# First-layer weight conversion on VectorE and ScalarE, even pieces for the band's values, and a new order of steps

## The chip, the core and the metric

One core of a Trainium2 chip runs the whole program. The metric is the device time of one execution in microseconds (us), as the median over several runs. The core has five engines that work through queues of their own, in order: TensorE (PE; its weight loads are listed as PEld), VectorE (DVE), ScalarE (ACT), GpSimd (POOL) and SyncE (SP), which here issues every DMA transfer. An instruction that waits holds up all that stand behind it on its engine.

## What is computed

The reference is an attention over two scales and two dense layers (the weights come as float64, all else as float32):

```python
# q, k, v: (4, 8, 576, 64)
q_d, k_d, v_d = means of 4 neighbours along the sequence      # 144 long
out = repeat(softmax(q_d k_d^T / 8) v_d, 4)                   # dense, pooled
    + softmax(q k^T / 8 where |i - j| < 4, else -1e9) v       # the band
x = out, heads side by side                                   # (2304, 512)
x = silu(x @ w_in) @ w_out                                    # 512 -> 2048 -> 512
x = h * sigmoid(1.702 h) @ w2_out,  h = x @ w2_in             # the same sizes
```

## The kernel before

**Stages.** The 2304 tokens are taken as eight half sequences of 288 (m = 0 to 7) in the first layer and as six blocks of 384 in the second. Attention is done in 32 *units*, one for each half sequence and pair of heads; four units (a half sequence) give the input of one first-layer block. A unit goes PE (transposes of q and k, L946 and L913; scores `sl`, L965 and L971), DVE (L979 to L988), POOL (subtract the maximum, L994), ACT (exponentials, L1000 and L1004), DVE (sums, L1007 to L1015), POOL (divide, L1018), DVE (transpose, L1033), PE (`ul`, L1042 and L1048), ACT (L1054), DVE (`xf`, L1062 and L1063, and its maximum, L1066). After four units the input is split into two float16 halves, `xhl` (L682 on ACT, L685 on DVE).

**The dense layers.** Each product is made of three float16 matmuls. A block's first product goes to PSUM as `hps` (L605); ACT takes its tanh (L617), DVE multiplies (L620), ACT and DVE split the result (`g`, L624 and L627); the second product is `ops` (L718, for m = 0 L746 with additions by DVE in L760; second layer L780). All of block m = 0 waits for the first layer's weights.

**Weights.** A weight comes as the two 32-bit words of a float64. `conv` (L295 to L327) makes a float32 out of them on integers: ACT scales the high word (L302) and converts the low word (L306, into `z`), DVE shifts the high word left by 3 (L310), DVE takes the sign bit into the upper half of `z` (L315), and POOL adds the two as integers (L319). The first layer's weights go through in 16 pieces of 128 x 1024 words (`weights1`), the second layer's in 32 pieces of 128 x 512 (`weights2`), which also pass through DRAM. `halves` then makes the float16 halves: ACT the upper (L338), DVE the rest (L342).

**The band.** A block of 24 queries sees 32 keys. `first_key` moves the window of the first and last block inward at the edges, so there are three masks (`bigs`), and `load_vw` fetches the values in eight DMAs for each pair of heads: 12, 12, 2, 5, 5, 2, 5, 5 windows of 32 keys.

**Order.** Every step of the program is an entry of `Plan`. A table of digits, `PLACES`, sets the one global order in which the steps are written out; every engine then executes its share in that order. SP's DMAs stand in it too.

Of the kernel before, what the change touches and what calls it, by code (L numbers as in the profile page):

```python
# [19 lines left out]
NEG = -1.0e9  # L20
# [3 lines left out]
BAND = 4  # L24
TERMS = ((0, 0), (0, 1), (1, 0))
# [7 lines left out]
    "0e0h0i0l0k0n0s0t0v0u0I0L0w0M0T0W1y0f0o0r0O0g0m0x0J0N0P0S0Q0U0X0Y100Z15171c1g1o1A2c14161d1E13181e1f1l1k1n1m1p1B1C1F1H1M1W1N202i2p2r1K"
    "1U1O2m1J1T1P1Z2a2b2g2f2h2n2o2q2s2y2z2u2A2C2F2G2K2M2N2R2W313g3J4w5m6h6M8o2527495e2L2Q2O2V2Z30393c3z3K3L3S3P4b4i3T4K4N4X4Z33383e3r403I"
    "4k3R4f4z4A4U4G5g5x5G5N5Q5T6i5058525h5o5n5y5v5P5Z6063666e6q6j6u6D6J6L5W68626c6k6m6r6p6C6G6H6K6I6Q6X6N6Y71797a7E7J7N858s8v8X3o467A5f6y"
    "6z6w7v7B927t7y959U9W967c7i7p4T7d7j7q7F7M7L7T7O7Y8a8b8f8c8k8D8u8G8J8N9l7X81897r7U7Z888i8n8t8C8w8K8O8P8S8Q8V9g8Z9v9A9EaD8U9c909G8T9b8Y"
# [28 lines left out]
    "B8BeBhBiBkBpBjBlBmBnBuBwBoBrBsBtBvBx"
)


class Rec:
    pass  # L70

class Step:
    __slots__ = ("name", "eng", "dur", "fn", "deps", "succ", "keys", "alloc", "lock", "rank", "start", "end", "left", "n", "mb")


class Plan:


    def __init__(self, caps):
        self.steps, self.last, self.readers, self.tags, self.users = [], {}, {}, {}, {}
        self.soft = []
        self.caps = caps

    def add(self, name, eng, dur, fn, r=(), w=(), alloc=(), lock=False, mb=0.0, after=()):
        s = Step()
# [110 lines left out]
def kernel(ctx: ExitStack, tc: tile.TileContext, q, k, v, w1_in, w1_out, w2_in, w2_out, out):  # L198
# [1081 lines left out]
```

## Time and profile before

| | |
|---|---|
| median of 3 runs (lowest, highest) | 946.28 us (944.89, 947.38) |
| span of the profiled execution | 945.0 us |
| median less that span | 1.3 us |
| busy PE, DVE, ACT, POOL | 885.7, 501.2, 422.6, 167.4 us |

The profile is of one execution. A busy PE is one with a matmul under way; small matmuls overlap, so a busy PE can still be short of its full rate. The granted TensorE clock is given as a share of 2.4 GHz. A row of a line gives its count, busy time and mean duration; a row of the order of time gives start and duration.

### The profile page before, as it was taken

What the parts mean: (1) busy time and instruction counts of PE and PEld (TensorE: products, weight loads), DVE (VectorE), ACT (ScalarE), POOL (GpSimd) and SP (SyncE); (2) the same over time, 40 slices, a digit from 0 to 9 for tenths busy, and PEclk for the clock granted to TensorE, in tenths of its full rate; (3) what the DMA queues carried; (4) which work ended last, traced back from release to release, by engine and by line L of the source; (5) the groups of instructions that cost most, each with busy time, mean ns of one, the idle gap of its engine ahead of it and who ended that gap; (6) DMA issues with size and microseconds to landing.
All of it is one profiled execution on the core that took longest, in us unless ns stands there. A gap on an engine that the chain in (4) does not pass through costs nothing.

```text
span 945.0 us, 20792 instructions
## 1 busy us (share of the span) xinstructions
PE 885.7 (94%) x8926; PEld 592.3 (63%) x8926; DVE 501.2 (53%) x1033; ACT 422.6 (45%) x753; POOL 167.4 (18%) x165
## 2 busy tenths in 40 slices
PE   4567789999999999999999999999999999999998
PEld 2335566777777777777778776455455464554553
DVE  5789999885857728537372557506025043140230
ACT  4668776776765526334251356315023132240230
POOL 4645542435342102301100000000000000000000
PEclk9997799999999999999999999999999999999999
DMA  7885346566655121311050030000000000000001
GB/s 191 261 260 195 91 132 170 167 188 221 182 173 151 43 65 39 86 26 36 2 224 1 2 125 10 12 23 1 22 12 1 23 1 1 34 1 34 1 1 45
DMA packets 87228, 76.85 MB, mean 81 GB/s; under 512 B 66912, under 2 KB 71520, under 8 KB 86112
## 3 DMA queue, kind: packets, MB, share of 16 engines
q1 hardware_dynamic: 87136, 75.52, 26.6%
q8 instruction: 70, 1.15, 0.5%
q14 instruction: 22, 0.18, 0.1%
HBM read 62.39 MB, written 13.11 MB: 80 GB/s over the span
## 4 chain that ended last, share of the span: by engine, by line
PE 76%; DVE 13%; ACT 4%; DMA 3%; POOL 2%; issue 2%; SPq 0%; POOLq 0%; ACTq 0%; DVEq 0%
PE hps L605 34%; PE ops L780 20%; PE ops L718 16%; DMA st<-in_moe_w_in_dram 2%; PE ul L1048 1%; DVE z L315 1%; DVE win L342 1%; DVE g L627 1%; PE sl L971 1%; DVE tg L620 1%; PE ul L1042 1%; DVE wout L342 1%; PE sl L965 1%; DMA vraw<-in_v_dram 1%; ACT st L302 1%
## 5 line engine op out<-in xcount | busy, mean ns | idle before, releaser
L605 PE MATMUL hps<-xhl,win 128*128 128x288 f16 (+1 forms) x2688 | 399.7, 309 | 12.3 <-DVE tg L620 10.4
L605 PEld LDWEIGHTS <-win 128*128 128x128 f16 x2688 | 264.3, 100 | 130.7 <-issue 11.2
L620 DVE SCALAR_TENSOR_TENSOR tg<-tg,hps 128x576 f32<-128x576 f32 (+1 forms) x112 | 93.3, 833 | 237.6 <-ACT tg L617 237.5
L780 PE MATMUL ops<-wout,g 128*128 128x512 f16 x864 | 187.8, 379 | 0.0
L718 PE MATMUL ops<-g,wout 128*128 128x288 f16 x1344 | 169.7, 286 | 1.0 <-DVE tg L620 1.0
L718 PEld LDWEIGHTS <-wout 128*128 128x128 f16 x1344 | 130.2, 98 | 33.8 <-DVE tg L620 1.4
L617 ACT ACTIVATE tg<-hps,blk 128x576 f32<-128x576 f32 (+1 forms) x112 | 90.6, 808 | 132.5 <-PE hps L605 126.9
L780 PEld LDWEIGHTS <-g 128*128 128x128 f16 x864 | 84.5, 98 | 100.9
L791 ACT ACTIVATE o<-ops,blk 128x512 f32<-128x512 f32 x18 | 12.4, 687 | 155.2 <-PE ops L780 155.2
L627 DVE SCALAR_TENSOR_TENSOR g<-tg,g 128x768 f16<-128x768 f32 (+1 forms) x56 | 51.0, 924 | 13.9 <-ACT g L624 13.8
L624 ACT ACTIVATE g<-tg 128x768 f16<-128x768 f32 (+1 forms) x56 | 44.8, 814 | 27.3 <-DVE tg L620 27.3
L319 POOL TENSOR_TENSOR cs<-cs,cz 128x512 int32<-128x512 int32 x32 | 43.2, 1354 | 51.1 <-DVE cz L315 18.8
L627 DVE SCALAR_TENSOR_TENSOR g<-tg,gs,g 128x576 f16<-128x576 f32 x56 | 48.0, 864 | 6.5 <-ACT g L624 6.5
L624 ACT ACTIVATE g<-tg,gs 128x576 f16<-128x576 f32 x56 | 42.5, 769 | 7.9 <-DVE tg L620 7.9
L319 POOL TENSOR_TENSOR x<-x,z 128x1024 int32<-128x1024 int32 x16 | 41.0, 2568 | 23.1 <-DVE x L310 7.0
L994 POOL TENSOR_TENSOR sc<-sc,mx 128x192 f32<-128x192 f32 x32 | 18.7, 584 | 148.6 <-DVE mx L988 146.1
L302 ACT ACTIVATE st<-st 128x512 f32<-128x512 f32 (+1 forms) x48 | 39.5, 827 | 9.3 <-DMA st<-in_moe_w_in_dram 7.3
L1018 POOL TENSOR_TENSOR sc<-sc,smr 128x192 f32<-128x192 f32 x32 | 23.0, 719 | 82.4 <-DVE smr L1012 76.9
L1000 ACT ACTIVATE pd<-sl,nm 72x144 f32<-72x144 f32 x64 | 23.5, 371 | 31.2 <-DVE sc L985 25.2
L728 ACT ACTIVATE x<-ops,blk 128x576 f32<-128x576 f32 x14 | 10.3, 738 | 40.5 <-PE ops L718 40.5
L1054 ACT ACTIVATE us<-ul 128x288 f32<-128x288 f32 x32 | 13.1, 409 | 34.2 <-PE ul L1048 34.0
L746 PE MATMUL ops<-g,wout 128*128 128x288 f16 x192 | 26.7, 294 | 1.6 <-DVE x L760 1.0
(122 smaller groups left out, 845.8 us busy)
## 6 DMA issues: line engine op xcount, KB each, us to landing
st<-in_moe_w_in_dram SPq DMA_DIRECT2D x8, 1024.0 KB, 7.5
st<-in_moe_w_out_dram SPq DMA_DIRECT2D x8, 1024.0 KB, 5.0
st<-in_moe_w_in_dram SPq DMA_DIRECT2D x16, 512.0 KB, 4.5
st<-in_moe_w_out_dram SPq DMA_DIRECT2D x16, 512.0 KB, 5.8
vraw<-in_v_dram SPq DMA_DIRECT2D x16, 288.0 KB
kraw<-in_k_dram SPq DMA_DIRECT2D x32, 144.0 KB, 4.0
qraw<-in_q_dram SPq DMA_DIRECT2D x64, 72.0 KB, 3.2
out_dram<-o SPq DMA_DIRECT2D x18, 256.0 KB, 2.0
```

The costliest lines, as they stand in the source:

```text
L302: ACT.activation(out=hi.bitcast(F32), in_=hi.bitcast(F32), func=AF.Copy, scale=2.0 ** -112)
L319: POOL.tensor_tensor(out=s, in0=s, in1=zget(), op=ALU.add)
L605: nc.tensor.matmul(o, T[w][:, kc, a, fc * P:(fc + 1) * P], T[xk][:, kc, b, :T_], start=(n == 0), stop=(n == 3 * KC - 1))
L617: ACT.activation(out=T[tg], in_=T[ps][:, :, :T_], func=AF.Tanh, scale=T["a" + bk][:, c:c + 1])
L620: DVE.scalar_tensor_tensor(out=T[tg], in0=T[tg], scalar=1.0, in1=T[ps][:, :, :T_], op0=ALU.add, op1=ALU.mult)
L624: ACT.activation(out=T[g][:, 0], in_=T[tg], func=AF.Copy, scale=gs)
L627: DVE.scalar_tensor_tensor(out=T[g][:, 1], in0=T[tg], scalar=gs, in1=T[g][:, 0], op0=ALU.mult, op1=ALU.subtract)
L718: nc.tensor.matmul(o, w[:, j, a, dc * P:(dc + 1) * P], g[:, b, j % 2, :], start=(n == 0), stop=(n == 3 * NF - 1))
L746: nc.tensor.matmul(T[ps][:, i, :HALF], T[f"wout1.{c}"][:, j, a, dc * P:(dc + 1) * P], g[:, b, j % 2, :], start=(n == 0), stop=(n == 11))
L780: nc.tensor.matmul(o, g[:, a, j % 2, t * P:(t + 1) * P], w[:, j, b, :], start=(i == 0), stop=(i == 3 * NF - 1))
L1000: ACT.activation(out=T[pd][:, hh, :], in_=sd()[:, hh, :], func=AF.Exp, bias=T[nmx][:, hh:hh + 1], scale=SCD, accum_out=T[sr][:PD, 6 + hh:7 ...
L1018: POOL.tensor_tensor(out=scu(), in0=scu(), in1=T["smr"][u % 2][:, 0:6].unsqueeze(2).to_broadcast([P, 6, 32]), op=ALU.mult)
```

## The change

For the first layer's weights the sign bit is taken by ACT (`sg`: the scaled high word, which is tiny, is written as float16, where only the sign is left) in place of DVE's `cg`, and the integer add is made by DVE (`cd`) in place of POOL's `cp`. The second layer keeps the old way. The keys in SBUF get 4 columns of zeros at either end, so that every window starts at its regular place; one mask is enough, and the cap's two edge blocks are closed by two small memsets. The band's values come in four DMAs of 32 partitions x 12 windows (five for the first and last pair of heads, with a small memset by POOL). `PLACES` is a new table: all steps may stand elsewhere. The durations that the steps carry do not set the order; the table alone does.

```diff
+CONV = {"in": [("DVE", "ACT")] * 8, "out": [("DVE", "ACT")] * 8}
 PLACES = (
-    "000b020104050A030D1s0E1u211t0C0G1w23060p0q0y0z111i0B0K0V0R1b121h0F1a191z1x1I280H1q1r1G1Q1L291v1Y1X2w2d2B2I222l2D2v2H2J3b262T2U2Y3236"
+    "0008040103050j020O0S0B1x1C1m060m0U1F270l0J0N0R0V0W14090x0A0C170Z1b0t151c181e1h1l0y1k1z1o1D1s1L1f1Q1X1V231Z281j292b2p2k2r2x252Q2T2U2W2Y"
...
+        def sg():
+            hi, _, _ = words(stget())
+            l1 = zget().bitcast(F16).rearrange("p (n w) -> p n w", w=2)[:, :, 1]
+            ACT.activation(out=l1, in_=hi.bitcast(F32), func=AF.Copy)
+
-        def cp():
+        def cp(eng):
             s = r().bitcast(I32)
-            POOL.tensor_tensor(out=s, in0=s, in1=zget(), op=ALU.add)
+            eng.tensor_tensor(out=s, in0=s, in1=zget(), op=ALU.add)
...
-        add("cg" + nm, "DVE", 0.17 + N / 1770.0, cg, r=[(key, "h"), (key, 0)], w=[z])
+        if sign == "ACT":
+            add("sg" + nm, "ACT", act(N) + 0.07, sg, r=[(key, "h"), (key, 0)], w=[z])
...
-        add("cp" + nm, "POOL", 0.15 + N * 0.00235, cp, r=[z], w=[rkey])
+        if by == "POOL":
+            add("cp" + nm, "POOL", 0.15 + N * 0.00235, lambda: cp(POOL), r=[z], w=[rkey])
+        else:
+            add("cd" + nm, "DVE", 0.16 + N * 0.00104, lambda: cp(DVE), r=[z], w=[rkey], lock=True)
...
-    def first_key(s):
-        return min(max(QB * s - BAND, 0), S - 32)
...
-        T["kTs"] = [ac.tile([P, S], F32, name=f"kT{i}") for i in range(NHP)]
+        T["kTs"] = [ac.tile([P, S + 2 * BAND], F32, name=f"kT{i}") for i in range(NHP)]
+        for t in T["kTs"]:
+            POOL.memset(t[:, 0:BAND], 0.0)
+            POOL.memset(t[:, BAND + S:], 0.0)
...
-        DVE.tensor_copy(out=cap[0:32, 0, :], in_=bigs[0][0:32, 0, :])
-        DVE.tensor_copy(out=cap[96:128, 2 * NBL - 1, :], in_=bigs[2 * BAND][96:128, 3, :])
+        DVE.memset(cap[0:32, 0, 0:BAND], 8.0 * NEG)
+        DVE.memset(cap[96:128, 2 * NBL - 1, 32 - BAND:], 8.0 * NEG)
...
-            win(1, first_key(1), 0, NE)
-            win(2, first_key(2), 0, NE)
-            for i, lo, edge in ((0, 1, 0), (3, 0, last)):
-                win(i, first_key(4 * edge + i), edge, 2, NE // 2)
-                for hh in range(2):
-                    win(i, hh * S + first_key(4 * lo + i), hh * NE // 2 + lo, last)
+            for i in range(4):
+                lo, hi = int(head and i == 0), NE - int(tail and i == 3)
+                win(i, lo, hi - lo)
```

Three places of the order show what the new table does. On DVE, the second piece of weights (`st` are staged weight words, `x_80` holds the converted words, `z` the low words with the sign; L408, the old L398, and the lines with `nm`, `sc`, `mx`, `smr`, `xf`, `qd` and `kd` belong to attention units). Before:

```order
L310 TENSOR_SCALAR x_80<-st_188 128x1024
L315 TENSOR_SCALAR z<-st_188 128x1024
L979 TENSOR_REDUCE nm<-sl 72x2
L980 TENSOR_SCALAR nm<-nm 72x2
L985 TENSOR_TENSOR sc<-sl,cap 128x192
L988 TENSOR_REDUCE mx<-sc 128x6
L310 TENSOR_SCALAR x_80<-st_286 128x1024
L1062 TENSOR_TENSOR xf<-ul_351,us 128x3x24
L1062 TENSOR_TENSOR xf<-ul_352,us 128x3x24
L1063 TENSOR_TENSOR xf<-ul_353,us 128x2x3x24
```

After, where the third piece is shifted and the second and third are added (L324 is the integer add, L352 the old L342, L1090 the old L1066):

```order
L310 TENSOR_SCALAR x_80<-st_275 128x1024
L1090 TENSOR_REDUCE blk<-xf 128x1
L324 ISA x_80<-x_80,z 128x2048
L352 SCALAR_TENSOR_TENSOR win_0_413<-x_80,bin_88,win_0_413 128x2x512
L1039 TENSOR_TENSOR pd<-pd,smr_165 72x288
L324 ISA x_80<-x_80,z 128x2048
L310 TENSOR_SCALAR x_80<-st_281 128x1024
L978 TENSOR_REDUCE qd<-qps 128x72
L944 TENSOR_REDUCE kd<-kps 128x144
```

L315, the sign, is gone from DVE; L324 has come, one for each piece. L310 writes the shifted word, and L324 follows it, at times behind the next piece's L310.

On DVE again, the stretch that ends with the first block's `xhl`, which the first `hps` waits for (`blk` and `wi` hold maxima). Before:

```order
L1063 TENSOR_TENSOR xf<-ul_732,us 128x2x3x24
L1066 TENSOR_REDUCE blk<-xf 128x1
L315 TENSOR_SCALAR z<-st_659 128x1024
L674 TENSOR_REDUCE blk<-rm 128x1
L262 TENSOR_SCALAR blk<-blk 128x1
L263 TENSOR_SCALAR blk<-blk 128x1
L264 RECIPROCAL blk<-blk 128x1
L954 TENSOR_REDUCE qd<-qps 128x72
L342 SCALAR_TENSOR_TENSOR win_0_589<-x_80,bin_88,win_0_589 128x2x512
L685 SCALAR_TENSOR_TENSOR xhl<-xf,blk,xhl 128x4x288
L310 TENSOR_SCALAR x_80<-st_670 128x1024
L310 TENSOR_SCALAR x_80<-st_675 128x1024
```

After (L688 and L699 are the old L674 and L685, L978 the old L954; L408 and L1003 to L1012 are the reduction of scores and the maxima of further units):

```order
L688 TENSOR_REDUCE blk<-rm 128x1
L262 TENSOR_SCALAR blk<-blk 128x1
L263 TENSOR_SCALAR blk<-blk 128x1
L264 RECIPROCAL blk<-blk 128x1
L654 TENSOR_SCALAR blk<-ibin_87,blk 128x1
L408 TENSOR_REDUCE wi_101<-sps 128x1
L1003 TENSOR_REDUCE nm<-sl 72x2
L1004 TENSOR_SCALAR nm<-nm 72x2
L1009 TENSOR_TENSOR sc<-sl,cap 128x192
L1012 TENSOR_REDUCE mx<-sc 128x6
L978 TENSOR_REDUCE qd<-qps 128x72
L699 SCALAR_TENSOR_TENSOR xhl<-xf,blk,xhl 128x4x288
```

Three halves of `win` stand ahead of `xhl` before, six after; the last integer add ahead of it, the seventh of the eight for `w_in`, stands three rows above this piece. A further unit's maxima and reductions of q and the pooled scores now stand between the block's maximum and `xhl`.

On SP, the loads that follow the first piece of weights (`kraw`, `qraw`: keys and queries of a pair of heads; `vraw` and `vw`: its values, pooled and for the band). Before:

```order
L859 DMA vraw<-in_v_dram 72x4x256
L480 DMA st_286<-in_moe_w_in_dram 128x2x1024
L891 DMA vw<-in_v_dram 32x12x64 x2
L891 DMA vw<-in_v_dram 32x2x64
L891 DMA vw<-in_v_dram 32x5x64 x2
L891 DMA vw<-in_v_dram 32x2x64
L891 DMA vw<-in_v_dram 32x5x64 x2
L855 DMA kraw<-in_k_dram 96x6x64 x2
L876 DMA qraw<-in_q_dram 96x3x64 x2
L480 DMA st_303<-in_moe_w_in_dram 128x2x1024
```

After:

```order
L869 DMA vraw<-in_v_dram 72x4x256
L490 DMA st_248<-in_moe_w_in_dram 128x2x1024
L903 DMA vw<-in_v_dram 32x11x64
L903 DMA vw<-in_v_dram 32x12x64 x3
L903 DMA vw<-in_v_dram 28x64
L490 DMA st_275<-in_moe_w_in_dram 128x2x1024
L490 DMA st_281<-in_moe_w_in_dram 128x2x1024
L886 DMA qraw<-in_q_dram 96x3x64 x2
L865 DMA kraw<-in_k_dram 96x6x64 x2
L869 DMA vraw<-in_v_dram 72x4x256
```

The third and fourth piece of weights now stand ahead of the third pair of heads.

## Rows read from the trace of the kernel before

**Rows 1.** Busy time by stretch: length, PE, PEld, DVE, ACT, POOL, PE clock, DMA share, GB/s.

```profile
0.00:20.00 20.00, 7.09 (x126) 5.11 (x127) 11.06 (x26) 7.86 (x15) 9.81 (x28) 1.00 0.75 199
20.00:61.00 41.00, 24.52 (x431) 16.10 (x432) 33.18 (x71) 26.05 (x45) 22.97 (x16) 1.00 0.87 259
61.00:100.00 39.00, 28.52 (x251) 18.87 (x251) 36.40 (x59) 27.03 (x41) 20.45 (x11) 0.81 0.54 175
100.00:140.00 40.00, 33.51 (x470) 24.83 (x468) 36.98 (x86) 32.65 (x58) 19.71 (x11) 0.89 0.43 118
140.00:192.00 52.00, 48.41 (x765) 37.72 (x767) 48.69 (x120) 37.70 (x85) 20.14 (x21) 1.00 0.60 169
192.00:460.00 268.00, 262.47 (x3765) 206.77 (x3766) 167.39 (x410) 140.97 (x322) 71.43 (x75) 1.00 0.38 106
460.00:941.00 481.00, 481.00 (x3123) 282.90 (x3121) 167.49 (x267) 149.66 (x190) 2.89 (x4) 1.00 0.07 28
```

**Rows 2.** Who waited for whom on PE, 60 to 200 us: total, times, longest.

```profile
PE hps L605 <- DVE tg L620: 10.4, 3, 3.9
```

**Rows 3.** The same for PE from 0 to 60 us.

```profile
PE tps L1025 <- DVE pd L1015: 8.1, 2, 4.6
PE kps L913 <- POOL smr L836: 5.4, 1, 5.4
```

**Rows 4.** DVE's groups from 0 to 192 us: busy, mean ns, idle before.

```profile
L315 DVE TENSOR_SCALAR z<-st 128x1024 uint16<-128x1024 uint16 x16 | 19.5, 1220 | 2.1 <-ACT z L306 1.4 <-ACT st L302 0.7
L342 DVE SCALAR_TENSOR_TENSOR win<-x,bin,win 128x1024 f16<-128x1024 f32 x8 | 17.7, 2222 | 0.0
L310 DVE TENSOR_SCALAR x<-st 128x1024 int32<-128x1024 int32 x16 | 11.8, 752 | 1.8 <-ACT st L302 1.8
...
L342 DVE SCALAR_TENSOR_TENSOR wout<-x,bout,wout 128x1024 f16<-128x1024 f32 x8 | 10.1, 1303 | 0.0
...
L315 DVE TENSOR_SCALAR cz<-st 128x512 uint16<-128x512 uint16 x9 | 6.1, 674 | 0.9 <-DMA qraw<-in_q_dram 0.9
...
L310 DVE TENSOR_SCALAR cs<-st 128x512 int32<-128x512 int32 x9 | 4.2, 464 | 0.0
```

**Rows 5.** Line 315's instructions: shortest, median, longest in ns, first and last start.

```profile
L315 DVE TENSOR_SCALAR z<-st x16: 733/836/2505, 17.4 to 116.5; 128x1024 uint16<-128x1024 uint16 x16
```

**Rows 6.** Order of time, 53 to 61 us, DVE and POOL: start, duration.

```profile
53.16 2.35 POOL L319 TENSOR_TENSOR x<-x,z 128x1024 int32<-128x1024 int32 x1 [4.44 <-PE sps L519]
...
53.79 2.33 DVE L315 TENSOR_SCALAR z<-st 128x1024 uint16<-128x1024 uint16 x1
...
56.26 2.35 POOL L319 TENSOR_TENSOR x<-x,z 128x1024 int32<-128x1024 int32 x1 [0.75 <-DVE blk L674]
...
57.01 2.69 DVE L342 SCALAR_TENSOR_TENSOR win<-x,bin,win 128x1024 f16<-128x1024 f32 x1
...
59.62 1.41 DVE L685 SCALAR_TENSOR_TENSOR xhl<-xf,blk,xhl 128x1152 f16<-128x1152 f32 x1
```

**Rows 7.** POOL's groups from 0 to 192 us.

```profile
L319 POOL TENSOR_TENSOR x<-x,z 128x1024 int32<-128x1024 int32 x16 | 41.0, 2568 | 23.1 <-DVE x L310 7.0 <-PE sps L519 6.2 <-DVE z L315 3.4
...
L1018 POOL TENSOR_TENSOR sc<-sc,smr 128x192 f32<-128x192 f32 x12 | 9.5, 791 | 21.4 <-DVE smr L1012 19.4 <-DVE wsm L412 1.7 <-DVE wsm L262 0.4
L994 POOL TENSOR_TENSOR sc<-sc,mx 128x192 f32<-128x192 f32 x12 | 8.0, 669 | 28.2 <-DVE mx L988 25.7 <-DVE blk L640 2.5
```

**Rows 8.** ACT's groups from 0 to 192 us.

```profile
L302 ACT ACTIVATE st<-st 128x1024 f32<-128x1024 f32 x16 | 18.1, 1133 | 6.6 <-DMA st<-in_moe_w_in_dram 6.6
```

**Rows 9.** Busy time from 20 to 140 us, columns as in rows 1.

```profile
20.00:140.00 120.00, 86.55 (x1151) 59.80 (x1151) 106.56 (x213) 85.73 (x143) 63.12 (x38) 0.90 0.62 185
```

**Rows 10.** SP's issues in order of time: start, time until the next can be issued.

```profile
8.84 9.96 SPq L891 DMA_DIRECT2D vw<-in_v_dram  x8
```

**Rows 11.** Order of time on DVE: the twelfth unit's maximum.

```profile
186.95 0.45 DVE L1066 TENSOR_REDUCE blk<-xf 128x1 f32<-128x288 f32 x1
```

More of the change, by code (lines that the diff above doesn't have):

```diff
@@ L33 @@
[L33 to L36, printed above, removed]
@@ L74 @@
 class Step:
-    __slots__ = ("name", "eng", "dur", "fn", "deps", "succ", "keys", "alloc", "lock", "rank", "start", "end", "left", "n", "mb")
+    __slots__ = ("name", "eng", "dur", "fn", "deps", "succ", "keys", "alloc", "lock", "rank", "start", "end", "left", "n", "mb", "nd")
 class Plan:
@@ L293, in words, with conv @@
         return w[:, :, 1], w[:, :, 0], h[:, :, 3]
-    def conv(L, kd, c, j, n, key, rkey, r, alloc, stget, zget, zalloc):
+    def conv(L, kd, c, j, n, key, rkey, r, alloc, stget, zget, zalloc, sign="DVE"):
         N = n * 512
@@ L325, in conv @@
         add("cs" + nm, "DVE", dve(N, True), cs, r=[(key, "h"), (key, 0)], w=[rkey], alloc=alloc, lock=True)
-        add("cg" + nm, "DVE", 0.17 + N / 1770.0, cg, r=[(key, "h"), (key, 0)], w=[z])
+        if sign == "ACT":
+            add("sg" + nm, "ACT", act(N) + 0.07, sg, r=[(key, "h"), (key, 0)], w=[z])
+        elif sign == "POOL":
+            add("cq" + nm, "POOL", 0.15 + N * 0.00105, lambda: cg(POOL), r=[(key, "h"), (key, 0)], w=[z])
+        else:
+            add("cg" + nm, "DVE", 0.17 + N / 1770.0, cg, r=[(key, "h"), (key, 0)], w=[z])
         return nm, N, cp, z
@@ L506, in zget @@
             return T[k]
[L508 removed]
+        by, sign = CONV[kd][2 * c + j // 2]
+        nm, N, cp, z = conv(L1, kd, c, j, 2, key, rkey, r, [], lambda: T[key].rearrange("p j e -> p (j e)"), zget, "st", sign)
         if kd == "in":
@@ L563, in weights2 @@
         nm, N, cp, z = conv(L2, kd, c, j, 1, key, ck, r, [("cs", ck)], lambda: T[key], zget, "cz")
-        add("cp" + nm, "POOL", 0.15 + N * 0.00235, cp, r=[z], w=[ck])
+        add("cp" + nm, "POOL", 0.15 + N * 0.00235, lambda: cp(POOL), r=[z], w=[ck])
         abs_sum(L2, kd, c, j, 1, ck, r)
@@ L885, in f, with win, z @@
         def f():
[L886 to L888 removed]
+            if vk not in T:
+                T[vk] = pools["ld"].tile([P, NE, D], F32, tag="vw", name="vw", bufs=4)
+            def win(i, e0, n, cut=0, rows=32):
+                k0 = QB * i - BAND + TT * e0 + cut
                 base = v.offset + ((b * H + 2 * hp) * S + k0) * D
[L891 to L903 removed]
+                nc.sync.dma_start(out=T[vk][32 * i + cut:32 * i + cut + rows, e0:e0 + n],
+                                  in_=bass.AP(v.tensor, base, [[D, rows], [TT * D, n], [1, D]]))
+            head, tail = b == 0 and hp == 0, b == B - 1 and hp == NHP - 1
+            for i in range(4):
+                lo, hi = int(head and i == 0), NE - int(tail and i == 3)
+                win(i, lo, hi - lo)
+            if head:
+                win(0, 0, 1, BAND, 32 - BAND)
+            if tail:
+                win(3, NE - 1, 1, 0, 32 - BAND)
+        if (b, hp) in ((0, 0), (B - 1, NHP - 1)):
+            r, e = (slice(0, 32), 0) if hp == 0 else (slice(96, 128), NE - 1)
+            def z():
+                T[vk] = pools["ld"].tile([P, NE, D], F32, tag="vw", name="vw", bufs=4)
+                POOL.memset(T[vk][r, e], 0.0)
+            add("z" + vk, "POOL", 0.3, z, w=[vk], alloc=[("vw", vk)])
+            s = add(vk, "SP", 0.44, f, w=[vk], mb=0.92)
+            plan.users[vk].append(s)
+        else:
+            s = add(vk, "SP", 0.44, f, w=[vk], alloc=[("vw", vk)], mb=0.92)
+        s.nd = 5 if (b, hp) in ((0, 0), (B - 1, NHP - 1)) else 4
     def keys_of(b, hp):
@@ L915, in cpy @@
         def cpy():
-            ACT.copy(out=T["kTs"][hp].rearrange("p (c t) -> p c t", c=2), in_=T[kps][:, :, :HALF])
+            ACT.copy(out=T["kTs"][hp][:, BAND:BAND + S].rearrange("p (c t) -> p c t", c=2), in_=T[kps][:, :, :HALF])
         def pool():
```

106 lines of the change are left out of this document (50 added, 56 removed).

## The prediction

> **What bounds the kernel now.** I read the busy times by stretch first, then who waited for whom on PE, then DVE's groups. PE is busy 481.0 of 481 us from 460 us on and 262.5 of 268 from 192 to 460 [rows 1]: nothing can be won there but 5.5 us. Up to 192 us it is idle 12.9, 16.5, 10.5, 6.5 and 3.6 us in the five stretches, 50.0 in all, and the granted clock is 0.81 in the third and 0.89 in the fourth, which costs 28.5 x 0.19 + 33.5 x 0.11 = 9.1 us of its full rate. So up to 59 us of PE are lost ahead of 192, and 5.5 behind it. The reader is to see next that DVE is the fullest of the others there: 166.3 of 192 us, with 16.8 of its 25.7 idle us ahead of 61, and 122.1 of 131 (93%) from 61 to 192. PE's waits agree: 10.4 us of `hps` for DVE's L620 behind 60 us [rows 2], 8.1 of a transpose for DVE's L1015 ahead of it [rows 3]. L620 does little itself; it stands in a full queue. The first `hps` starts when DVE's `xhl` ends, 59.62 + 1.41 = 61.03 us [rows 6].
>
> **The sign leaves DVE.** Sixteen L315 of mean 1220 ns are 19.5 us [rows 4]; the shortest is 733, the median 836, the longest 2505 [rows 5]. The long ones lie beside POOL's add: 2.33 us from 53.79 beside an L319 from 53.16 to 55.51 [rows 6]. All of it goes: **-19.5**.
>
> **The add comes to DVE.** The trace of before has no integer add on DVE. The cheapest row with as many words is the shift, L310, 752 ns, with one input: 16 x 0.75 = 12.0 us below. POOL's own add of the same words is 2568 ns [rows 7]: 41.1 us above. Less than nothing is excluded, since DVE has 16 instructions where it had none of this kind. The nearest row is L342 on `wout`, 1303 ns, which reads two arrays of 1024 elements in SBUF and writes one, beside little of POOL's adds [rows 4]. I take 1.30: **+20.8**. The Trainium skill ("VectorE: DVE Perf Modes", "The perf-mode tier table") gives a `tensor_tensor` of 2048 16-bit elements 1224 ns in its 2x mode and 2293 ns without it; the order lists the add as 2048 elements, so by the page it would be 19.6 us or 36.7 us.
>
> **POOL's add goes.** POOL loses 41.0 us that were on its own path only; what matters is what they did to DVE. L342 on `win` takes 2222 ns, on `wout` 1303 [rows 4]; the one at 57.01 lasted 2.69 us beside an L319 from 56.26 to 58.61 [rows 6]. With no L319 for these pieces I put `win` at 1303: 8 x 0.919 = **-7.4**. The bounds are nothing (should the slowness be `win`'s own) and -7.4. POOL's steps of the units, L994 and L1018, twelve each of 0.67 and 0.79 us, stay [rows 7]; beside them an add on DVE could still be stretched, by at most 24 x 0.73 = 17.5 us if each met one, which I hold for unlikely in more than a few cases. The Trainium skill ("SBUF — State Buffer", "Who interferes with whom") says that a DVE instruction with two SBUF inputs contends with a GpSimd instruction that reads SBUF, for the whole instruction. By it the add would still meet L994 and L1018; the trace agrees with the rule at 57.01 [rows 6].
>
> **Second-layer pieces are put off.** By the twelfth unit's maximum, which is at 186.95 us before [rows 11], DVE has done 8 shifts and 9 signs of the second layer in the old order, and 1 and 1 in the new: 7 x 0.464 + 8 x 0.674 = **-8.6** [rows 4]. They come back later, where DVE is busy 167.4 of 268 us [rows 1]; that cover makes them free. Were it gone, 8.6 us would come back.
>
> **Sum on DVE** up to that point: -19.5 + 20.8 - 7.4 - 8.6 = -14.7 us. Four L620 and five L627 also fall behind that point; they are only late, and I don't count them.
>
> **Where on the way.** Up to the first `xhl` the new order has on DVE 7 adds, three more halves of `win`, two more shifts, and a good deal of one further unit (2.7 us), while six signs go (and 1.4 us of other maxima): 7 x 1.30 + 3 x 1.30 + 2 x 0.75 + 2.7 - 6 x 1.22 - 1.4 = +8.5 us. So I expect the first `hps` near 69.5 us instead of 61.1. Behind it DVE has about 122 - 14.7 - 8.5 = 99 us up to the old 192, and PE 110.4 us of matmuls, 101 at the full clock [rows 1]. DVE stops being the fuller one there. That is what the gain rests on: PE's loss behind the first `hps`, now 20.6 idle and 9.1 by the clock = 29.7 us, must shrink by more than 8.5.
>
> **ACT** gets 16 signs. The nearest row is L302, 1133 ns for as many elements [rows 8]: +18.1, in the way of every add, since the add needs the sign. From 20 to 140 us ACT is busy 85.7 of 120 [rows 9]. I let four of the sixteen delay DVE: 4.5 us. DVE's own idle share of 7% takes 1.0 of the 14.7. Together I give back **6**.
>
> **The band.** One mask for three, eight tiny memsets on POOL and two small copies turned into memsets on DVE lie in the first 5 us, where a `kps` waits 5.4 us for POOL's L836 [rows 3]: I price them at 0, within 1 us either way. `vw` goes in 4 or 5 issues instead of 8 with the same bytes. The first eight took SP 9.96 us from 8.84 [rows 10], and the third piece of weights is queued behind them. Fewer issues are worth between nothing (if the time is that of the bytes) and some 4 us of earlier weights, which DVE's full queue doesn't need; I take 0. On SP the third and fourth piece now stand ahead of the third pair of heads, whose keys and queries so come later; that costs PE units at the start and is in the 8.5.
>
> **The rivals.** *PE pays for the late first product.* From 140 us on PE is busy 48.4 of 52 us and then full, so what DVE saves there doesn't reach the end. Speaking for it: the first `hps` comes 8.5 us later, and the work that PE can do instead is one further unit. If the loss behind it falls from 29.7 to 25 only, the span is 945.0 + 8.5 - 4.7 = 948.8, the median **950**: slower. The point from which it decides is a loss of 21.2 us (29.7 - 8.5) between the first `hps` and the end of the old 192 us. Against it: DVE's 99 us to PE's 101 there.
>
> *The add costs as much as on POOL.* At 2.57 us the sum is -14.7 + 16 x 1.27 = +5.6, and with 6 given back +11.6; DVE's idle 16.8 us ahead of 61 take a few, so **955**. It decides from 1.30 + 8.7 / 16 = 1.84 us each. Against it: no DVE row of 1024 elements takes that long alone.
>
> *ACT becomes the bound.* 85.7 + 18.1 = 103.8 of 120 us on ACT from 20 to 140, against 106.6 on DVE [rows 9]: the two would be level, and DVE's sum counts for little, some 3 us of gain: **943.5**. Against it: ACT's steps there are not all before DVE's.
>
> *It does more than I think.* With adds at 0.75 us the sum is -23.5, less 6: **928.5**.
>
> **How the numbers follow.** -14.7 + 6 = -8.7, so 945.0 - 8.7 = 936.3 for the span; the median is 1.3 above the profiled span, 937.6, and I write 937. A measurement of this kernel tells some 0.3% (2.8 us) from no change, so "same" is 943.4 to 949.1. The forecast (931 to 942) has 0.52, the larger gain 0.07, ACT as the bound 0.15, the late product 0.18, the dear add 0.08. Faster: 0.50 + 0.07 + 0.05 of the ACT case = 0.62. Same: 0.02 + 0.10 + 0.05 of the late product = 0.17. Slower: 0.13 + 0.08 = 0.21. The range from 927 to 951 takes in the cheap add and the late product and leaves out the dear add and ends of the others, under 2 in 10.
>
> **What would show it.** The first `hps` between 66 and 72 us; the add's mean at 1.2 to 1.5 us; L342 on `win` near 1.3; DVE's busy sum up to the twelfth unit's maximum some 15 us lower and that maximum near 178 us; PE's idle time up to there below 42 us and the granted clock nearer to 1. Wrong would make it: an add above 1.84 us, a first `hps` behind 75 us, waits of DVE's L324 for ACT of more than 10 us in all, or a PE that waits again behind 192 us, for the second layer's pieces.

## The result and the profile after

The changed kernel takes 930.30 us (median of 4 runs, 928.83 to 931.69), the kernel before, run beside it, 946.38: a ratio of 0.9822, 95% interval 0.9801 to 0.9843. It is 16 us faster; 9 were forecast, and the time lies inside the range of 927 to 951. The profiled execution has a span of 929.8 us against 945.0, so the two spans differ by 15.2, and the sums below are made against that.

First the busy times by stretch of the kernel after, columns as in [rows 1]: length, PE, PEld, DVE, ACT, POOL with their counts, granted clock of PE, DMA share, GB/s.

```profile
0.00:20.00 20.00, 7.37 (x126) 5.09 (x126) 9.17 (x25) 7.79 (x14) 6.80 (x30) 1.00 0.99 225
20.00:61.00 41.00, 20.00 (x370) 12.90 (x371) 35.25 (x69) 32.50 (x50) 11.24 (x11) 1.00 1.05 264
61.00:100.00 39.00, 31.69 (x526) 22.13 (x525) 33.83 (x82) 35.35 (x63) 7.06 (x10) 1.00 0.55 159
100.00:140.00 40.00, 36.02 (x492) 27.39 (x496) 36.26 (x93) 35.92 (x60) 8.44 (x8) 0.83 0.55 139
140.00:192.00 52.00, 51.79 (x788) 40.57 (x790) 43.21 (x107) 30.17 (x65) 11.35 (x13) 1.00 0.26 67
192.00:460.00 268.00, 267.67 (x3875) 212.82 (x3876) 167.81 (x422) 146.84 (x329) 70.03 (x78) 1.00 0.41 109
...
0.00:69.90 69.90, 33.41 (x612) 21.55 (x612) 52.20 (x113) 48.54 (x76) 18.55 (x41) 1.00 0.97 240
...
20.00:140.00 120.00, 87.71 (x1388) 62.42 (x1392) 105.35 (x242) 103.78 (x171) 26.73 (x28) 0.94 0.72 188
```

The reader is to see four things. The stretch 140 to 192 is full (51.8 of 52 us of PE, 48.4 before), and so is 192 to 460 (267.7 of 268, 262.5 before). The clock is down in one stretch only, 0.83 from 100 to 140, where it was 0.81 and 0.89 in two. POOL has fallen from 63.1 [rows 9] to 26.7 us between 20 and 140, ACT has risen from 85.7 to 103.8, and DVE stands nearly still, 106.6 and 105.4. And PE has lost time ahead of its first product: 33.4 us busy in the first 69.9.

Then the groups that answer to [rows 4, 7, 8], from 0 to 192 us: busy, mean ns, idle time before them.

```profile
L324 DVE CUSTOM_DVE_ANT_0 x<-x,z 128x2048 uint16<-128x2048 uint16 x16 | 20.2, 1266 | 1.6 <-ACT z L320 1.5
L310 DVE TENSOR_SCALAR x<-st 128x1024 int32<-128x1024 int32 x16 | 13.2, 822 | 1.3 <-ACT st L302 1.2
...
L352 DVE SCALAR_TENSOR_TENSOR win<-x,bin,win 128x1024 f16<-128x1024 f32 x8 | 10.4, 1330 | 0.0
L352 DVE SCALAR_TENSOR_TENSOR wout<-x,bout,wout 128x1024 f16<-128x1024 f32 x8 | 10.1, 1278 | 0.0
...
L315 DVE TENSOR_SCALAR cz<-st 128x512 uint16<-128x512 uint16 x1 | 0.8, 772 | 0.0
...
L320 ACT ACTIVATE z<-st 128x1024 f16<-128x1024 f32 x16 | 21.6, 1358 | 0.1
```

The add is the custom instruction of L324, 1266 ns. `win`'s L352 has come down from 2222 to 1330 ns, as fast as `wout`'s. Of the second layer's signs one is left in this stretch. The new sign on ACT takes 1358 ns, more than L302's 1133.

The order of time around the first product (start, duration; `xhl`, then the first `hps`):

```profile
68.37 1.52 DVE L699 SCALAR_TENSOR_TENSOR xhl<-xf,blk,xhl 128x1152 f16<-128x1152 f32 x1
...
71.62 1.65 PE L619 MATMUL hps<-xhl,win 128*128 128x288 f16 x6
```

`xhl` ends at 69.89 us, where before it ended at 61.03 [rows 6].

### The profile page after: what moved, and what is told of

It reads as the page before. It is cut to its first block, busy times and chain, and to the rows that moved or that the text cites. A ratio compares the mean times of both kernels' runs of the same rounds, so it can differ in the third digit from the quotient of the medians.

```text
span 929.8 us, 20704 instructions
## 1 busy us (share of the span) xinstructions
PE 880.5 (95%) x8926; PEld 591.9 (64%) x8926; DVE 487.8 (52%) x1033; ACT 440.5 (47%) x769; POOL 122.5 (13%) x153
## 4 chain that ended last, share of the span: by engine, by line
PE 88%; DVE 5%; ACT 4%; DMA 2%; issue 1%; POOL 0%; SPq 0%; DVEq 0%
PE hps L619 39%; PE ops L794 20%; PE ops L732 18%; PE ops L760 2%; PE ul L1072 2%; PE sl L995 2%; DMA st<-in_moe_w_in_dram 1%; PE sl L989 1%; PE ul L1066 1%; PE tps L1049 1%; ACT z L320 1%; DVE x L324 1%; PE qps L970 1%; PE kps L937 1%; PE sps L530 1%
## 5 line engine op out<-in xcount | busy, mean ns | idle before, releaser
L619 PE MATMUL hps<-xhl,win 128*128 128x288 f16 (+1 forms) x2688 | 393.3, 306 | 0.2 <-DVE tg L634 0.2
L805 ACT ACTIVATE o<-ops,blk 128x512 f32<-128x512 f32 x18 | 12.4, 687 | 155.5 <-PE ops L794 155.5
L324 POOL TENSOR_TENSOR cs<-cs,cz 128x512 int32<-128x512 int32 x32 | 41.5, 1299 | 111.1 <-DVE cs L310 27.1
L641 DVE SCALAR_TENSOR_TENSOR g<-tg,gs,g 128x576 f16<-128x576 f32 x56 | 45.6, 824 | 6.5 <-ACT g L638 6.2
L302 ACT ACTIVATE st<-st 128x512 f32<-128x512 f32 (+1 forms) x48 | 39.3, 824 | 1.3 <-DMA st<-in_moe_w_in_dram 1.3
L1024 ACT ACTIVATE pd<-sl,nm 72x144 f32<-72x144 f32 x64 | 23.5, 371 | 27.1 <-DVE sc L1009 12.8
L1086 DVE TENSOR_TENSOR xf<-ul,us 128x72 f32<-128x72 f32 x64 | 11.8, 225 | 33.3 <-ACT us L1078 33.3
L989 PE MATMUL sl<-kd,qd 64*72 64x144 f32 x128 | 16.9, 344 | 11.0 <-DVE qd L978 8.6
L950 POOL TENSOR_TENSOR vraw<-vraw 72x512 f32<-72x512 f32 x16 | 22.1, 1379 | 31.8 <-DMA vraw<-in_v_dram 31.8
```

The costliest lines, as they stand in the source:

```text
L302: ACT.activation(out=hi.bitcast(F32), in_=hi.bitcast(F32), func=AF.Copy, scale=2.0 ** -112)
L324: eng.tensor_tensor(out=s, in0=s, in1=zget(), op=ALU.add)
L619: nc.tensor.matmul(o, T[w][:, kc, a, fc * P:(fc + 1) * P], T[xk][:, kc, b, :T_], start=(n == 0), stop=(n == 3 * KC - 1))
L641: DVE.scalar_tensor_tensor(out=T[g][:, 1], in0=T[tg], scalar=gs, in1=T[g][:, 0], op0=ALU.mult, op1=ALU.subtract)
L989: nc.tensor.matmul(sd[:, hh, :], T[qd][r, :], T[kd][r, :], start=True, stop=True)
L1024: ACT.activation(out=T[pd][:, hh, :], in_=sd()[:, hh, :], func=AF.Exp, bias=T[nmx][:, hh:hh + 1], scale=SCD, accum_out=T[sr][:PD, 6 + hh:7 ...
```

## The experiments

Each run stands against the kernel before run beside it on the same chip; "after" is the changed kernel. All differences in us below are between the medians. Two theories were to be told apart at first: **the sum on DVE** (the prediction's: DVE's queue is the bound, what it is given or spared goes to the end), and that the **order** or the **conversions** alone make the gain.

### All but the order, the band alone, the order with the old conversions

The first (e1) is the changed code with the steps in the old order:

```diff
 PLACES = (
-    "0008040103050j020O0S0B1x1C1m060m0U1F270l0J0N0R0V0W14090x0A0C170Z1b0t151c181e1h1l0y1k1z1o1D1s1L1f1Q1X1V231Z281j292b2p2k2r2x252Q2T2U2W2Y"
+    "000b020104050A030E1t0F1v221u0C0D0H1x24060p0q0y0z121j0B0L0W0S1c131i0G1b1a1A1y1J290I1r1s1H1R1M2a1w1Z1Y2x2e2C2J232m2E2w2I2K3c272U2V2Z3337"
...
```

> The changed code (add on DVE, sign on ACT, band and value loads new) in the old order of steps. Theory 'sum on DVE': the conversions alone are worth -19.5 + 20.8 - 7.4 = -6.1 us on DVE, so about 941 us (938 to 944). Rival 'the order alone makes the gain': no change, 946 (944 to 948). Rival 'the conversions alone make the gain': 933 or less.

Measured: 943.63 us, ratio 0.9962 (0.9947 to 0.9976), at the upper edge of the theory's range. The second (e2) has the old order and the old conversions, so that the mask, the cap and the value loads alone are new:

```diff
-CONV = {"in": [("DVE", "ACT")] * 8, "out": [("DVE", "ACT")] * 8}
+CONV = {"in": [("POOL", "DVE")] * 8, "out": [("POOL", "DVE")] * 8}
```

> The old order and the old conversions (add on POOL, sign on DVE); only the band's mask, cap and value loads are new. Theory 'sum on DVE': priced at 0, so 945 to 948 us. Rival 'SP's fewer issues bring the weights earlier': some 4 us less, 942.

Measured: 946.09 us, ratio 0.9980 (0.9967 to 0.9994). The third (e3) has that same line, in the new order.

> The changed kernel with the conversions put back (add on POOL, sign on DVE), in the new order. Theory 'sum on DVE': of the gain only the second layer's put-off pieces are left, -8.6 us of DVE, less what the POOL adds of 2.57 us cost in places cut for adds of 1.27: 939 to 946, I take 942. Rival 'the order alone makes the gain': 930 to 934. Rival 'order and conversions only work together': 946 or more.

Measured: 942.09 us, ratio 0.9953 (0.9938 to 0.9968). So in the old order the conversions are worth 946.1 - 943.6 = 2.5 us, in the new one 942.1 - 930.3 = 11.8. The new order with the old conversions is worth 946.1 - 942.1 = 4.0. The two don't simply add up: of the 15.8 us between e2 and after, 9.3 come only of both together. Where the conversions meet a limit in the old order can be looked for in e1 by stretch (columns as above):

```profile
30.00:62.00 32.00, 16.47 (x276) 10.81 (x271) 27.72 (x62) 25.82 (x39) 6.30 (x8) 0.50 1.13 265
70.00:100.00 30.00, 19.63 (x183) 13.99 (x181) 28.28 (x54) 29.97 (x40) 5.82 (x5) 0.89 0.56 180
```

ACT is busy 29.97 of 30 us from 70 to 100, as one rival said, but DVE is busy 28.28 of them too. What ACT takes back is seen better in DVE's waits for it. Added up from 0 to 192 us they are 10.9 us in e2 and 19.4 in e1, while DVE's busy time falls from 168.3 to 160.2: the 8.1 us that the conversions spare DVE are waited away. In the new order these waits don't grow (17.4 in e3, 16.2 in after). Two of e1's rows, who waited for whom on DVE up to 140 us (total, times, longest; L325 is the add, L321 the sign):

```profile
DVE x L325 <- ACT z L321: 4.9, 3, 2.8
DVE smr L1032 <- ACT sc L1029: 2.8, 1, 2.8
```

No run changes ACT's share alone in the old order, so this is a reading and not shown by an experiment. PE also ran at 0.50 of its full clock, 1.2 GHz, from 30 to 62 us, busy 16.5 of 32 us there; at the full clock that work is 8.2 us less. The record speaks against this as the cause: the six executions of e1 had mean clocks from 0.966 to 0.989, and the one at 0.989 took 944.05 us, the two fastest 941.7 at 0.976 and 0.978. The time of e3 is the one that the theory named, 942, but e6 below shows that it comes about in another way.

The trace of e3 shows what POOL's add does to DVE, and not only to long instructions. Order of time in e3, POOL, DVE and ACT around some of POOL's adds:

```profile
23.50 2.36 POOL L324 TENSOR_TENSOR x<-x,z 128x1024 int32<-128x1024 int32 x1 [1.91 <-PE sps L530]
...
24.25 1.64 DVE L1035 TENSOR_SCALAR smr<-smr 128x8 f32<-128x8 f32 x1
...
29.25 3.04 DVE L352 SCALAR_TENSOR_TENSOR win<-x,bin,win 128x1024 f16<-128x1024 f32 x1
...
33.10 3.00 POOL L324 TENSOR_TENSOR x<-x,z 128x1024 int32<-128x1024 int32 x1 [1.90 <-DVE z L315]
33.21 0.69 DVE L310 TENSOR_SCALAR x<-st 128x1024 int32<-128x1024 int32 x1
...
38.95 2.79 DVE L1004 TENSOR_SCALAR nm<-nm 72x2 f32<-72x2 f32 x1
39.38 2.33 POOL L324 TENSOR_TENSOR x<-x,z 128x1024 int32<-128x1024 int32 x1
...
41.85 0.38 ACT L1024 ACTIVATE pd<-sl,nm 72x144 f32<-72x144 f32 x1 [2.04 <-DVE nm L1004]
```

An L1035 on 8 elements lasts 1.64 us and ends at 25.89, when the add ends (25.86); an L1004 on 2 elements lasts 2.79 us, to 41.74, when the add that has started meanwhile ends (41.71), and an exponential on ACT waits 2.04 us for it. Not every instruction is held: the L310 at 33.21 lasts its usual 0.69 us, and it is the add beside it that takes 3.00 us in place of some 2.35. An add at 47.98 even takes 4.43, beside two L352 of their normal length. The groups of before (there L980 and L1011), of e3, and of after, from 0 to 192 us:

```profile
L980 DVE TENSOR_SCALAR nm<-nm 72x2 f32<-72x2 f32 x12 | 5.0, 415 | 0.4
...
L1011 DVE TENSOR_SCALAR smr<-smr 128x8 f32<-128x8 f32 x12 | 3.3, 272 | 0.4
```

```profile
L1035 DVE TENSOR_SCALAR smr<-smr 128x8 f32<-128x8 f32 x13 | 9.3, 716 | 1.1 <-DVE smr L1031 0.5 <-ACT pd L1024 0.3
...
L1004 DVE TENSOR_SCALAR nm<-nm 72x2 f32<-72x2 f32 x14 | 6.7, 481 | 0.5
```

```profile
L1004 DVE TENSOR_SCALAR nm<-nm 72x2 f32<-72x2 f32 x15 | 2.6, 176 | 0.5
L1035 DVE TENSOR_SCALAR smr<-smr 128x8 f32<-128x8 f32 x14 | 2.4, 168 | 0.7 <-ACT pd L1024 0.3
```

These two small steps stand in every attention unit's chain, so the stretching hits PE's units twice: in DVE's sum (11.0 us between e3 and after) and as latency. In the kernel before the stretching of these two was 12 x (415 - 176) + 12 x (272 - 168) ns = 4.1 us.

### The value loads

e4 cuts the outer windows of the changed kernel's loads into short pieces again:

```diff
-                win(i, lo, hi - lo)
+                if i in (1, 2):
+                    win(i, lo, hi - lo)
+                else:
+                    edges = sorted({lo, hi} | {e for e in (1, 6, 7, 11) if lo < e < hi})
+                    for e0, e1 in zip(edges, edges[1:]):
+                        win(i, e0, e1 - e0)
```

> The changed kernel, in which the band's values come in eight pieces for each pair of heads again (12, 12, and 1, 5, 1, 5 or the like for the outer ones) instead of four, the same bytes to the same places. Theory 'sum on DVE': no change against the changed kernel, 930 to 931 us. Rival 'SP's issues hold up the weights': 3 to 4 us more, 934.

That makes twelve issues for each pair of heads and not the eight of the kernel before, six of them of one window. Measured: 938.33 us, ratio 0.9912 (0.9896 to 0.9928), 8.0 us more than after. So e5 was made with the old eight:

```diff
-            for i in range(4):
...
-                win(i, lo, hi - lo)
+            for i in (1, 2, 0, 3):
+                if i in (1, 2):
+                    win(i, 0, NE)
+                    continue
+                first, rest = (0, 1) if i == 0 else ((NE // 2) - 1, 0)
...
+                    win(i, first, 2, step=(NE // 2))
+                win(i, rest, (NE // 2) - 1)
+                win(i, (NE // 2) + rest, (NE // 2) - 1)
```

> The changed kernel with the band's values in the eight issues of the kernel before (12, 12, 2, 5, 5, 2, 5, 5 windows) for each pair of heads; e4 had twelve issues for most pairs, not eight, and cost 8 us. Theory 'SP's issues hold up the weights behind them': half of e4's added issues, so 3 to 5 us, 933 to 935. Rival 'only very short transfers (one window) cost': 930 to 931.

Measured: 929.65 us, ratio 0.9809 (0.9788 to 0.9830): no difference from after; 3 to 5 us were expected, a miss. SP's issues in order of time (start, us until the next can be issued), the last weight piece of `w_in` in after, e5 and e4:

```profile
45.83 0.39 SPq L490 DMA_DIRECT2D st<-in_moe_w_in_dram  x1
```

```profile
52.29 0.39 SPq L490 DMA_DIRECT2D st<-in_moe_w_in_dram  x1
```

```profile
59.54 0.39 SPq L490 DMA_DIRECT2D st<-in_moe_w_in_dram  x1
```

This piece goes out at 45.83, 52.29 and 59.54 us; the times are 930.3, 929.7 and 938.3. A delay of 6.5 us is covered, one of 13.7 costs 8.0. That fits some 6 us of slack for the weights in the new order, which would be why the changed loads earn nothing there, but it isn't shown by itself: the rate of the DMAs from 20 to 61 us in e4 is 198 GB/s against 264 in after, `xhl` ends 3.8 us later, and PE loses 2.9 us more behind 192 (264.8 us busy to 460, 267.7 in after). What about the one-window transfers is slow wasn't taken apart.

### The order alone

e6 is e5 with e3's line: old conversions and old issues in the new order.

> The new order alone: old conversions (add on POOL, sign on DVE) and the old eight issues of the band's values, only the mask and the cap remain new. Theory 'order and parts add up': e3's 942 and what e5 costs, 945 to 947: the order by itself is worth nothing. Rival 'the order alone makes a part of the gain': 940 to 942.

Measured: 941.87 us, ratio 0.9939 (0.9918 to 0.9961): 5.0 us less than before, where the theory expected nothing and the rival 940 to 942; the mask and the cap can have at most a part of e2's 1.7 in it. Its stretch from 192 to 460, and that of e2 with the old order:

```profile
192.00:460.00 268.00, 267.67 (x3886) 212.49 (x3884) 170.91 (x429) 148.15 (x333) 69.98 (x78) 1.00 0.40 109
```

```profile
192.00:460.00 268.00, 262.38 (x3764) 206.59 (x3763) 166.00 (x409) 140.68 (x322) 71.60 (x76) 1.00 0.39 105
```

PE's 5.5 us of idle time behind 192 are gone with the new order whatever the conversions are (267.3 to 267.7 in e3, in e6 to e10 and in e12), and are there with the old order whatever the conversions are (262.4 in e2, 262.5 in e1 and before). That part of the gain belongs to the order. In the kernel before it was made up of many short waits of PE for DVE and ACT, none above 1.2 us.

### One half of the conversion put back

e7 puts the sign back on DVE, e8 the add back on POOL, each alone:

```diff
-CONV = {"in": [("DVE", "ACT")] * 8, "out": [("DVE", "ACT")] * 8}
+CONV = {"in": [("DVE", "DVE")] * 8, "out": [("DVE", "DVE")] * 8}
```

> The changed kernel with only the sign put back on DVE (16 of some 0.78 us) and taken off ACT (16 of 1.36 us); the add stays on DVE. Theory 'sum on DVE': +12.5 us on DVE, so 940 to 943 us. Rival 'ACT is as full as DVE there' (103.8 and 105.4 of 120 us from 20 to 140): ACT's 21.7 us make up for it, 929 to 934.

```diff
-CONV = {"in": [("DVE", "ACT")] * 8, "out": [("DVE", "ACT")] * 8}
+CONV = {"in": [("POOL", "ACT")] * 8, "out": [("POOL", "ACT")] * 8}
```

> The changed kernel with only the add put back on POOL (2.57 us each); the sign stays on ACT. Theory 'sum on DVE': DVE loses 20.2 us and gets back at most the 7.4 us by which POOL's adds stretch its own instructions, so 918 to 926 us. Rival 'POOL's add stands in the chain of a piece and stretches DVE in turn': 1.3 us more in the chain of each of eight pieces ahead of the first product, and DVE no freer, 935 to 942.

Measured: e7 932.58 us, ratio 0.9838 (0.9811 to 0.9865); e8 933.39 us, ratio 0.9857 (0.9830 to 0.9884). Busy times from 20 to 140 us, of e7, then e8:

```profile
20.00:140.00 120.00, 85.40 (x1362) 60.94 (x1363) 110.79 (x257) 87.07 (x157) 31.27 (x28) 0.94 0.72 189
```

```profile
20.00:140.00 120.00, 86.56 (x1368) 61.86 (x1368) 95.07 (x226) 102.17 (x169) 60.91 (x43) 0.93 0.71 186
```

The sum on DVE falls with both: it forecast 940 to 943 for e7 and 918 to 926 for e8. e7's time lies in its rival's range, e8's just below its rival's 935 to 942. e7 has 5.4 us more on DVE than after in this stretch and costs 2.3; e8 has 10.3 us less on DVE and is not faster but slower by 3.1. Each half brings most of the gain by itself: from e3 to e7 (add moved) 9.5 us, from e3 to e8 (sign moved) 8.7, both 11.8 (by the ratios 10.9, 9.1 and 12.4, since the kernel before took 947.8 beside e3 and 946.9 beside e7 and e8). Put back alone, a half costs 2 to 3 us; put back together, 11.8. The 2 to 3 us are near the limit of what can be told apart: the intervals of both ratios overlap that of after (0.9801 to 0.9843).

### What a microsecond costs on each engine

e9 adds a shift by nothing behind each add on DVE, e10 repeats half of ACT's signs:

```diff
             eng.tensor_tensor(out=s, in0=s, in1=zget(), op=ALU.add)
+            if eng is DVE and N == 1024:
+                DVE.tensor_single_scalar(out=s, in_=s, scalar=0, op=ALU.logical_shift_left)
```

> The changed kernel with a second DVE instruction behind each integer add (a shift by 0 bits over the same words, some 0.72 us): an add of 2.0 us, above the 1.84 us at which the prediction saw no gain left. Theory 'sum on DVE': +11.5 us, 940 to 943 us. Rival 'DVE has slack in the new order' (e7 put 12.8 us back on DVE and lost 2 to 3): 931 to 936.

```diff
             ACT.activation(out=l1, in_=hi.bitcast(F32), func=AF.Copy)
+            if j == 0:
+                ACT.activation(out=l1, in_=hi.bitcast(F32), func=AF.Copy)
```

> The changed kernel with the sign's ACT instruction made twice in 8 of the 16 pieces (it writes the same again): 8 x 1.36 = 10.9 us more on ACT. Theory 'sum on DVE': ACT has room, 930 to 933 us. Rival 'ACT and DVE are level in the new order': either one costs about the same, so as much as e9 costs for its 11.5, within 2 us. Rival 'ACT is the bound': 938 to 941, and e9 cheap.

What they add, from 0 to 192 us, e9, then e10:

```profile
L326 DVE TENSOR_SCALAR x<-x 128x1024 int32<-128x1024 int32 x16 | 12.7, 791 | 0.5
```

```profile
L322 ACT ACTIVATE z<-st 128x1024 f16<-128x1024 f32 x8 | 10.8, 1356 | 0.3
```

Measured: e9 939.36 us, ratio 0.9912 (0.9880 to 0.9945); e10 939.77 us, ratio 0.9910 (0.9878 to 0.9943). 12.7 us on DVE cost 9.1, 10.8 on ACT cost 9.5. Neither engine has room for that much, and a us costs about as much on the one (0.7) as on the other (0.9), as the first rival in e10's expectation said; in this sense the two are level. The sum on DVE comes near in e9, where DVE alone is touched, and fails in e10. It fits that e7 is cheap: it gives ACT back 21.6 us while DVE takes 12.8. One rival stays untested. Both runs also make each piece's own way longer, and DVE's waits for the sign rise from 1.5 us in after to 8.4 in e10; no run separates the longer way from the fuller engine.

### The second layer's pieces early, and a mixed sign

e11 moves the loads, conversions and stores of the first eight second-layer pieces of the changed kernel back to where the old order had them among the other steps.

```diff
 PLACES = (
...
-    "5D6g6J7e787h7o4U5S6y667P7V8e64707L7y7T7Z895o5y5F5J6i6F6M6N6W6P6V6X72757k7q7D7I7v7E7G7M7R7W8283868l8m8q8u8y8B8F8D8H9q0e0g0f0d0b0h0i0k0o"
+    "5D6g6J7e787h7p4U5S6y667P7V8s64707L7y7T818f5o5y5F5J6i6F6M6N6W6P6V6X72757l7r7D7I7w7E7G7M7R7Y84858b8z8A8J8N8R8U8Z8W909V0e0g0f0d0b0h0i0k0o"
...
```

> The changed kernel in which the first eight second-layer pieces (loads, ACT's, DVE's and POOL's steps and stores) stand again as early among the other steps as in the old order; five of them come ahead of the twelfth unit's maximum in place of one. Theory 'sum on DVE': 4 x (0.46 + 0.67) = 4.5 us of DVE come back, 933 to 935 us. Rival 'ACT's share of these pieces counts too' (2.2 us of ACT each): 936 to 941. Rival 'they are covered at either place': 929 to 931.

Measured: 963.87 us, ratio 1.0174 (1.0138 to 1.0211), 33.6 us more than after, far outside all three. Who waited for whom on SP's queue in e11 from 0 to 192 us (total, times, longest; L581 are the stores of converted pieces, L870 the loads of `vraw`, L561 those of second-layer weights):

```profile
SPq L581 <- POOL cs L325: 15.4, 5, 11.2
SPq L870 <- POOL vd L952: 15.4, 5, 8.4
...
SPq L561 <- DVE cs L311: 12.2, 2, 8.0
```

The wait of L870 is as long in after (15.1 us, there L869). New are the stores, none of which stands ahead of 192 us in after: SP stands still behind them while they wait for pieces not yet converted, and a pair of values queued behind them goes out at 176.4 us, in after at 157.0. So the run doesn't price the 8.6 us of DVE for which it was made: that term is left open. What it does show is that the place of these pieces can cost far more than their share of DVE's sum; DVE's busy time up to 192 us is even lower, 140.2 against 157.7. That SP's queue is the way it costs is read from these waits and wasn't tested.

e12 puts the sign of every other `w_out` piece back on DVE:

```diff
-CONV = {"in": [("DVE", "ACT")] * 8, "out": [("DVE", "ACT")] * 8}
+CONV = {"in": [("DVE", "ACT")] * 8, "out": [("DVE", "DVE"), ("DVE", "ACT")] * 4}
```

> The changed kernel with the sign of every other w_out piece (4 of 16) back on DVE. Theory 'sum on DVE': +3.1 us on DVE, 932 to 934 us. Rival 'ACT and DVE are level': -5.4 us on ACT and +3.1 on DVE, 928 to 930, a little better than the changed kernel.

Measured: 931.26 us, ratio 0.9822 (0.9788 to 0.9855): the same as after. It lies between the two ranges and decides for neither. No version was found that beats it; e5's 929.65 is within the measurement of it.

## Why the prediction was right, and where its size was off

**By PE's books.** The forecast was a first product 8.5 us later and a loss behind it, now 29.7 us, that shrinks by 8.5 + 8.7 = 17.2. Measured: up to 69.9 us PE was idle 69.9 - 33.4 = 36.5 us, 7.1 more than up to 61 before. From there to 192 it was idle 122.1 - 113.5 = 8.6, and the clock of 0.83 costs 36.0 x 0.17 = 6.1: 14.7 us, so the loss shrank by 15.0. Both terms are right within 2.5 us. Behind 192 the idle time went from 5.5 to 0.3 us: -5.2. The rest, 15.2 - (15.0 + 5.2 - 7.1) = 2.1 us, lies in PE's busy time (885.7 to 880.5, of which 3.0 are the clock's and counted above). To count the clock as lost time is bookkeeping only. In the executions of the kernel before that ran beside e1 the time doesn't follow the mean clock: those at 0.969 took 944.6 to 949.5 us, those at 0.991 took 946.2 to 949.4.

**The step that failed in size** is the first one: "nothing can be won there but 5.5 us" was written of the time behind 192, and then none of it was entered in the sum. All but 0.3 came. It belongs to the new order (e6 against e2), which the prediction priced only by what it does to DVE's sum ahead of 192; "the order by itself" had no term. With it the forecast would have been 937 - 5 = 932.

**Signs that failed.** The twelfth unit's maximum ended at 168.4 us (187.4 before); it was put near 178. PE's idle time up to it is 45.1 us and not below 42. DVE's busy time up to it fell by 24.0 us, from 161.9 to 137.9, and not by 14.7. Of that, 7.0 us are the nine L620 and L627 that the prediction set aside as only late, and 7.0 are three small steps that are shorter now: L980 (5.0 to 2.1 us), L1011 (3.3 to 2.0) and L374 (3.9 to 1.1). The prediction looked for POOL's effect in `win` alone. The new order moves that maximum among the steps, so its time doesn't measure the gain.

**The add**: 1.30 us taken, 1.27 measured. **`win`**: 1.303 taken, 1.330 measured; the whole 7.4 us (7.3) came. **The sign on ACT**: 1133 ns taken from L302, 1358 measured, so 21.6 us and not 18.1. The nearest row had the same elements but another output: L302 writes every second 32-bit word, the sign every second 16-bit half. **The first product**: 69.5 forecast, `xhl` ended at 69.9, and `hps` began at 71.6, because the units' scores and a transpose that waits for DVE's L1039 stand ahead of it on PE. **Waits of L324 for ACT**: 1.5 us, far below the 10 that would have told against it.

**The band's loads** were priced at 0 with DVE's full queue as the cover. e5 shows 0 in the new order, and e4 shows the cover's end. In the old order the band's part is worth 1.7 us (e2, ratio 0.9980), with the mask, the cap and the loads not told apart. **The second layer's pieces**: not settled, see e11.

**From a sum on DVE to a time.** The rule behind the forecast, that DVE's us go one for one to the end, is wrong in both directions. DVE's busy time up to 192 us is 164.5 in e7 and 160.0 in e3, and e7 is the faster by 9.5. What the experiments show in its place is two things. POOL's adds hold some of DVE's instructions until they end (e3), small ones in the units' chains too, which the prediction counted only for `win`; and in the new order a us on ACT costs about what one on DVE does (e9, e10). The signs' going to ACT is so worth less than DVE's sum says, and the add's leaving POOL is worth more. The errors offset each other: -14.7 + 6 came near to the truth ahead of 192 (-7.9 there, -13.1 with what lies behind) without being its mechanism, so that the time fell inside the range is in part luck. Two small slips are in the working: 4.5 + 1.0 makes 5.5 and not 6, and the rival with the cheap add comes to 928.8 and not 928.5.

**The rivals.** *PE pays for the late first product* set its point at a loss of 21.2 us behind the first `hps`; 14.7 were measured, so it fell. *The add costs as much as on POOL* fell at 1.27 us. Its point of no gain, 1.84 us each, was too low: at 1.25 + 0.79 = 2.04 in e9 the kernel is still 0.9912 of before. *ACT becomes the bound* forecast 103.8 us on ACT from 20 to 140, and 103.8 were measured (with a dearer sign and fewer other steps); its 943.5 is near what e1 took in the old order, where DVE's waits for ACT grow by 8.5 us, and in the new one ACT is level with DVE in the sense of e9 and e10.

**The shared port.** The prediction let the Trainium skill ("SBUF — State Buffer", "Who interferes with whom") speak for contention of DVE's two-input instructions with POOL's reads. e3 agrees for L352 (3.04 us from 29.25, beside an add from 28.55 to 31.21), and shows more: L1035 and L1004, `tensor_scalar` with one input, are held as well, to the end of POOL's add. The same section of the Trainium skill lists `tensor_scalar` among the operations that can take the shared pair of ports; the rows of 1.64 and 2.79 us above fit that, and the L310 that wasn't held at 33.21 shows that it doesn't happen each time. The Trainium skill ("VectorE: DVE Perf Modes", "The perf-mode tier table") gave 1224 ns for a `tensor_tensor` of the add's count of elements at its faster tier and 2293 at the slower; the trace has 1266 for the add, near the faster.

## What to carry to other kernels

When a step leaves an engine whose instructions hold up another's, as POOL's add did DVE's here, price what it did to the *small* instructions in long chains, not only to the large ones. A sum of one engine's busy time gives a time only as long as no second engine is as full: work out the neighbour's sum after the change, and where the two are level, take each us at less than one and look for what a change of order does by itself. An order that is changed together with the work gets its own term, read from the idle time of the bounding engine in each stretch, the late ones too.

## What was not expected of the hardware

POOL's integer add over 128 x 1024 words held a DVE `tensor_scalar` of 2 elements for 2.79 us, whose mean is 176 ns without it. In e1 PE's granted clock stood at 0.50 from 30 to 62 us and rose behind the first `hps` (0.86 from 60 to 70, 1.00 from 70 to 80), and yet e1's executions with the lower mean clocks were not the slower ones. Cutting the value loads into twelve pieces with some of one window lowered the DMAs' rate from 264 to 198 GB/s between 20 and 61 us, eight pieces only to 250.
